# Scores and some values of a windowed attention on array tiles of 64 rows by 32 columns

## Chip, cores and metric

The kernel runs on one core of one Trainium2 chip. The metric is the device time of one execution in microseconds (us), the median of several runs. Beside them one execution was profiled; its times are those of the trace. The engines are named as in the profile: PE is the matrix engine (PEld its weight loads), DVE the vector engine, ACT the scalar engine, POOL the general one, SP the one that issues most transfers.

## The reference

Two layers follow each other, for 8 batches of 576 positions. The first is causal attention with 8 heads of 64, in which each position sees itself and the 127 before it, with a slope per head that falls with the distance. The second is a gated network that mixes positions.

```
scores = q @ k.T / sqrt(64) - slope[h] * |i - j|     # q, k, v: 8 batches, 8 heads, 576 x 64
scores = where(0 <= i - j < 128, scores, -1e9)
x = softmax(scores) @ v                              # heads side by side: 576 x 512
h = gelu(x @ w_in); u, g = h[:, :512], h[:, 512:]
g = w_sg @ layernorm(g) + b_sg                       # over positions
out = x + (u * g) @ w_out
```

## The kernel before

The work of the attention is cut into 32 pairs of heads (class `Pair`, number n, four to a batch). A pair's 576 queries are nine blocks of 64 (R = 64). The operands of the products of the attention are 32-bit floats, and the trace has two weight loads and two products for each call of `nc.tensor.matmul` on them.

**Scores.** `qk` holds q and k transposed: the 64 numbers of head 0 on partitions 0 to 63, those of head 1 on 64 to 127. One product of `score` has 64 queries of one head as weights and the keys that they can see as the moving operand: 192 columns, 128 for the second block of queries, 64 for the first. So it uses 64 rows and 64 columns of the array of 128 by 128, a quarter ("64*64" in the profile). `score_list(t2)` makes eight products (i, half, j) for two banks of PSUM, `banks[half]`; head j goes to the partitions `heads[half ^ j]`, so that four products in a row lie on four different quarters. For t2 = 0 it appends the two products of the first block ("last products" below), which go to bank 0 as well. From pair 5 on, one step `*` issues both t2 = 0 (banks from the pool `ps_a`) and t2 = 2 (banks from `ps_s`): 18 products, 36 in the trace. Before that the steps `a` and `c` issue them apart. `burst` keeps the order in which the list has them.

**Minima.** For each bank DVE runs `minima` (steps A, B, C, G): `copy_predicated` (L302) merges the two halves of a diagonal block, and `shift` (helper line L295) adds the slopes and takes the minimum of a row. Step A, of the bank with the last products, comes first. ACT takes exponentials (L311), DVE the inverse sums, POOL or ACT scales, PE transposes (L347, L360), and DVE multiplies with the mask into `px` (L356).

**Values.** `values` (step V, L384 and L388) multiplies by v: `part(k, c)` for the nine blocks k of keys, and `first(c)` for the first block of queries, each for the two halves of the columns of v. Odd k use rows 0 to 63 of the array and bank `x1[0]`, even k rows 64 to 127 and bank `x1[1]`; the half c picks the columns. These are quarters too, 20 products, 40 in the trace. A product has 192 columns for k = 1 to 6, 128 for k = 0 and 7, 64 for k = 8 and for `first`. For the pairs in `BEHIND` (13 and 15 to 29) the result of `first` goes into a bank of the scores of pair n + 2, and the two `first` lie on different rows; for the other pairs from 4 on both lie on rows 0 to 63, and before that on rows 64 to 127. In the order of steps, the values of pairs 15 to 29 come directly behind the scores of pair n + 2 on PE; those of pair 13 have other products between.

**Order.** Each step runs where the string `ORDER` puts it, and every engine takes its instructions in that order; a `Planner` checks the buffers. The rest of PE's work is the gated network, in products on the whole array (128*128), of which most go to `ps_m` (two buffers).

## Time and profile before

| | |
|---|---|
| median of 3 runs | 577.24 us (577.07 to 577.51) |
| the profiled execution, its own time | 576.7 us |
| its span from first to last instruction | 575.0 us |
| instructions | 14661, of them 5495 products and 5495 weight loads on PE |

A product's duration in the trace runs from its issue to its last result, so neighbours overlap; PE's share of busy time says only that it has something in flight. How long a stretch takes is read from the start of its first product to the start of the first product of the next work.

### The profile page before, as it was taken

To read this page: it belongs to the slowest core of one execution; us is meant where nothing else is said; L and a number is where in the kernel's file an instruction comes from. 1 tells how busy PE (TensorE), PEld (TensorE's weight loads), DVE (VectorE), ACT (ScalarE), POOL (GpSimd) and SP (SyncE) were. 2 spreads that over 40 slices of the span, in tenths; PEclk is the share of its full clock that TensorE was granted. 3 is DMA by queue.
4 is the path that set the end of the run, shared out by engine and by line. 5 is a ranking of instruction groups with operands and counts; after the bars stand their busy time and mean duration, and the time that the engine had idled before them with its cause. 6 is when DMAs were issued, how large, how long until landed. Compare 5 with 4: busy or idle time off the path is not lost.

```text
span 575.0 us, 14661 instructions
## 1 busy us (share of the span) xinstructions
PE 560.0 (97%) x5495; PEld 510.0 (89%) x5495; DVE 474.0 (82%) x1324; ACT 378.3 (66%) x1063; POOL 307.2 (53%) x365
## 2 busy tenths in 40 slices
PE   5899999999999999999999999999999999999997
PEld 4677899998899789998999998998999999998997
DVE  8989998799989778999787987878897988575646
ACT  7998997466844867567777576646695666733422
POOL 3676646520436544575338753496348653576325
PEclk9899999999999999999999999999999999999999
DMA  8675213216404413554260554136431606012502
GB/s 301 194 231 200 79 57 104 68 68 224 166 38 149 133 38 99 163 186 120 65 218 1 166 180 175 42 103 183 124 112 65 216 1 198 2 39 93 172 1 82
DMA packets 43561, 69.78 MB, mean 121 GB/s; under 512 B 3554, under 2 KB 31202, under 8 KB 43492
## 3 DMA queue, kind: packets, MB, share of 16 engines
q1 hardware_dynamic: 43492, 68.86, 36.7%
q8 instruction: 43, 0.70, 0.5%
q14 instruction: 26, 0.21, 0.1%
HBM read 56.27 MB, written 12.58 MB: 120 GB/s over the span
## 4 chain that ended last, share of the span: by engine, by line
PE 89%; DVE 4%; ACT 4%; DMA 2%; issue 1%; POOL 0%; SPq 0%; DVEq 0%; ACTq 0%
PE ps_m L609 13%; PE ps_m L1061 13%; PE ps_m L611 12%; PE ps_m L610 12%; PE ps_m L907 12%; PE ps_a L347 5%; PE ps_a L278 4%; PE ps_s L278 4%; PE ps_m L384 3%; PE ps_s L384 3%; PE ps_m L942 2%; PE ps_m L943 2%; ACT e L311 1%; PE ps_m L798 1%; PE ps_m L800 1%; DMA wst<-w_in 1%
## 5 line engine op out<-in xcount | busy, mean ns | idle before, releaser
L334 POOL TENSOR_TENSOR e<-e,rr 128x256 f32<-128x256 f32 (+2 forms) x116 | 80.6, 717 | 96.4 <-DVE rr L323 84.0
L311 ACT ACTIVATE e<-e,stats 128x128 f32<-128x128 f32 (+1 forms) x288 | 110.7, 387 | 17.2 <-DVE stats L295 16.6
L224 POOL TENSOR_TENSOR region<-u,region 128x288 fp32r<-128x288 f32 (+1 forms) x78 | 77.7, 1016 | 44.5 <-ACT region L1008 16.2
L356 DVE TENSOR_TENSOR px<-ps_a,m_both 128x1024 f32<-128x1024 f32 x64 | 77.4, 1216 | 5.4 <-PE ps_a L347 4.7
L609 PE MATMUL ps_m<-ws,region 128*128 128x288 f32 x256 | 78.3, 306 | 0.0
L611 PE MATMUL ps_m<-ws,region 128*128 128x288 f32 x256 | 75.9, 296 | 0.0
L610 PE MATMUL ps_m<-ws,region 128*128 128x288 f32 x256 | 75.6, 295 | 0.0
L732 POOL TENSOR_TENSOR rs<-rs,mhalf 128x1 f32<-128x1 f32 (+1 forms) x40 | 30.2, 756 | 57.5 <-DVE rs L729 57.3
L218 POOL TENSOR_TENSOR xs<-xf,xs 128x288 fp32r<-128x288 f32 (+1 forms) x48 | 49.9, 1060 | 13.8 <-ACT xs L403 13.8
L311 ACT ACTIVATION_READ_ACCUMULATOR e<-e,stats 128x1 f32 x288 | 54.5, 189 | 0.0
L1008 ACT ACTIVATE region<-u 128x576 fp32r<-128x576 f32 x35 | 23.7, 684 | 43.1 <-PE ps_m L610 17.5
L609 PEld LDWEIGHTS ps_m<-ws,region 128*128 128x128 f32 x256 | 48.3, 189 | 1.6 <-issue 0.8
L610 PEld LDWEIGHTS ps_m<-ws,region 128*128 128x128 f32 x256 | 48.3, 189 | 0.1
L611 PEld LDWEIGHTS ps_m<-ws,region 128*128 128x128 f32 x256 | 48.1, 188 | 0.2 <-DVE region L744 0.2
L609 PE MATMUL ps_m<-wi,xs 128*128 128x512 f32 x112 | 46.7, 417 | 0.1
L1068 DVE TENSOR_TENSOR xf<-ps_m,xf 128x576 f32<-128x576 f32 x48 | 35.8, 750 | 10.4 <-PE ps_m L1061 9.7
L611 PE MATMUL ps_m<-wi,xs 128*128 128x512 f32 x112 | 44.3, 396 | 0.0
L610 PE MATMUL ps_m<-wi,xs 128*128 128x512 f32 x112 | 44.2, 395 | 0.0
L347 PE MATMUL ps_a<-ident,e 128*128 128x128 f32 x256 | 38.6, 277 | 1.0 <-DVE px L356 1.0
L948 DVE TENSOR_TENSOR u<-ps_m,u 128x576 f32<-128x576 f32 x32 | 24.0, 753 | 18.2 <-PE ps_m L943 11.6
L278 PE MATMUL ps_s<-qk 64*64 64x192 f32 (+2 forms) x576 | 32.2, 338 | 5.5 <-DMA qk<-qkT 4.6
L295 DVE CUSTOM_DVE_ANT_0 e<-ps_s,bias 128x128 f32<-128x128 f32 (+1 forms) x140 | 34.9, 287 | 2.5
(217 smaller groups left out, 1591.8 us busy)
## 6 DMA issues: line engine op xcount, KB each, us to landing
qk<-qkT SPq DMA_DIRECT2D x32, 576.0 KB, 4.9
sum<-store SPq DMA_DIRECT2D x36, 512.0 KB, 4.7
outT<-xf SPq DMA_DIRECT2D x31, 288.0 KB, 3.0
vt<-v_in SPq DMA_DIRECT2D x32, 256.0 KB, 4.2
wst<-w_in SPq DMA_DIRECT2D x8, 512.0 KB, 5.2
store<-sum SPq DMA_DIRECT2D x6, 512.0 KB, 2.8
vt<-v_in SPq DMA_DIRECT2D x64, 32.0 KB, 3.8
wst<-w_out SPq DMA_DIRECT2D x4, 512.0 KB, 3.6
```

What stands on the lines that cost most here:

```text
L218: (engine or nc.gpsimd).tensor_tensor(out[:, cs], a[:, cs], b[:, cs], op)
L224: nc.gpsimd.tensor_tensor(out[:, fs], a[:, fs], b[:, fs], ALU.subtract)
L278: return lambda: nc.tensor.matmul(banks[half][to, c:c + k1 - k0], qk[js, 0, q0:q0 + R], qk[js, 1, k0:k1], start=True, stop=True)
L311: nc.scalar.activation(x, x, AF.Exp, bias=self.nm[0:n, i:i + 1], scale=-1.0, accum_out=self.sm[0:n, i:i + 1])
L334: nc.gpsimd.tensor_tensor(x[:, z:z + step, :], y[:, z:z + step, :], self.rr[0:n, i + z:i + z + min(k, step)].rearrange("p (m o) -> p m o", ...
L347: burst([lambda t=t: nc.tensor.transpose(cv[:, t // 2, t % 2], self.pr[j][:, t, :].rearrange("p (h c) -> p h c", h=2), ident[:, j * R:j * ...
L356: nc.vector.tensor_tensor(xv, cv, mv, ALU.mult)
L609: nc.tensor.matmul(dst, ah, bh, start=(first and i == 0), stop=False)
L610: nc.tensor.matmul(dst, ah, bl, start=False, stop=False)
L611: nc.tensor.matmul(dst, al, bh, start=False, stop=(last and i == n - 1))
L907: nc.tensor.matmul(dst, left(n, g, c)[:, ms], right(n, h, c), start=first and c == 0 and k == 0, stop=c == 1 and k == 2, skip_group_check= ...
L1061: nc.tensor.matmul(dst, p, q, start=first and f == 0 and k == 0, stop=f == 1 and k == 2, skip_group_check=True)
```

## The change

`score` makes two products of each: 32 queries as weights, so 64 rows by 32 columns of the array, an eighth. The half z of a block sees the keys from `q0 + z - 128` (or 0) to `q0 + z + 32`, so the moving operand has 160 columns and not 192; the second block of queries has 96 and 128, and not 128. The 32 queries of z = 32 are put 32 columns further, so a band of scores is now 160 columns behind the one before it, and `minima` reads it through `window`, a pattern of two pieces, of the same sizes as before. For t2 = 0 the order is i = 1, then i = 0, and the last products are taken out of the list and issued at the end of the step's burst (in `*`, behind those of t2 = 2).

In `values` the pairs of `BEHIND` cut c in four, so each product has 32 columns of v as weights and the same moving columns as before; the other pairs keep quarters. The order of k is 1 to 7, then 0, and k = 8 is issued between the `first` products. Nothing else changes; the order of steps is the same.

```diff
     XW = 2 * S + R
+    BAND = 5 * R // 2
+    LEAD = 2 * BAND + R // 2
+
+    def window(bank, c0, c1):
+        x = bank[:, c0:c0 + R].rearrange("p (t c) -> p t c", t=1)
+        return bass.AP(tensor=x.tensor, offset=x.offset, ap=[x.ap[0], [c1 - c0, 2], x.ap[2]])
...
         def scores(self, *t2s):
-            burst([x for t2 in t2s for x in self.score_list(t2, ps_a if len(t2s) > 1 and t2 == 0 else ps_s)])
+            insts = [x for t2 in t2s for x in self.score_list(t2, ps_a if len(t2s) > 1 and t2 == 0 else ps_s)]
+            burst(insts + (self.last_scores if 0 in t2s else []))
...
-            def score(half, j, c, q0, k0, k1):
-                js, to = heads[j], heads[half ^ j]
-                return lambda: nc.tensor.matmul(banks[half][to, c:c + k1 - k0], qk[js, 0, q0:q0 + R], qk[js, 1, k0:k1], start=True, stop=True)
+            half_block = R // 2
+
+            def score(half, j, c, q, k0, k1):
+                js, to = heads[j], heads[half ^ j].start + q % R
+                return lambda: nc.tensor.matmul(banks[half][to:to + half_block, c:c + k1 - k0], qk[js, 0, q:q + half_block], qk[js, 1, k0:k1], start=True, stop=True)
 
             insts = []
-            for i in range(2):
+            for i in (1, 0) if t2 == 0 else (0, 1):
                 for half in range(2):
                     for j in range(2):
-                        q0 = (2 * t2 + 1 + i + 2 * half) * R
-                        if q0 < P:
-                            insts.append(score(half, j, i * W + R, q0, 0, P))
-                        else:
-                            insts.append(score(half, j, i * W, q0, q0 - P, q0 + R))
+                        for z in (0, half_block):
+                            q0 = (2 * t2 + 1 + i + 2 * half) * R
+                            lo = max(q0 + z - P, 0)
+                            insts.append(score(half, j, i * BAND + lo - q0 + P, q0 + z, lo, q0 + z + half_block))
             if t2 == 0:
-                insts += [score(0, j, 2 * W, 0, 0, R) for j in range(2)]
+                self.last_scores = [score(0, j, LEAD, z, 0, R) for j in range(2) for z in (0, half_block)]
             return insts
...
-            nc.vector.copy_predicated(sv[:, 0:6:5, :], sel_first if alone else sel, sv[:, 2:4, :])
+            nc.vector.copy_predicated(window(bank, 0, BAND + P), sel_first if alone else sel, window(bank, P, BAND))
...
-            WIDE = D
-            cols = [c for j in (1, 0) for c in range(j * D, (j + 1) * D, WIDE)]
-            burst([part(k, c) for k in (0, 1, 2 * T, *range(2, 2 * T)) for c in cols] + [first(c) for c in cols])
+            wide = D // 2 if behind else D
+            order = [*range(1, 2 * T), 0, 2 * T]
+            cols = [c for j in (1, 0) for c in range(j * D, (j + 1) * D, wide)]
+            burst([part(k, c) for k in order[:-1] for c in cols] + [x for c in cols for x in (first(c), part(2 * T, c))])
```

## Rows read from the trace of the kernel before

**Rows 1.** The page: busy time, share of the span and instructions of each engine.
```profile
PE 560.0 (97%) x5495; PEld 510.0 (89%) x5495; DVE 474.0 (82%) x1324; ACT 378.3 (66%) x1063; POOL 307.2 (53%) x365
```

**Rows 2.** The page: the chain that ended last, share of the span by engine.
```profile
PE 89%; DVE 4%; ACT 4%; DMA 2%; issue 1%; POOL 0%; SPq 0%; DVEq 0%; ACTq 0%
```

**Rows 3.** Waits of PE: us in total, times, longest; longest first.
```profile
PE ps_s L278 <- DMA qk<-qkT: 4.6, 1, 4.6
...
PE ps_a L347 <- DVE px L356: 1.0, 1, 1.0
```

**Rows 4.** Windows: length, then busy us (and instructions) of PE, PEld, DVE, ACT, POOL.
```profile
0.00:30.00 30.00, 21.29 (x220) 16.78 (x220) 25.93 (x112) 26.39 (x91) 15.69 (x27) 0.94 0.75 248
...
400.00:500.00 100.00, 100.00 (x992) 93.41 (x991) 82.05 (x238) 70.72 (x192) 51.52 (x77) 1.00 0.35 112
```

**Rows 5.** Timeline of PE, one step of scores: start, us, what, count.
```profile
229.14 0.29 PE L943 MATMUL ps_m<-wsB,vB 66*128 66x288 f32 x1
229.37 0.88 PE L278 MATMUL ps_a<-qk 64*64 64x128 f32 x20
230.08 0.82 PE L278 MATMUL ps_s<-qk 64*64 64x192 f32 x16
230.83 0.40 PE L609 MATMUL ps_m<-ws,region 128*128 128x288 f32 x1
```

**Rows 6.** Timeline of PE, scores with values directly behind.
```profile
253.02 0.88 PE L278 MATMUL ps_a<-qk 64*64 64x128 f32 x20
...
254.38 1.48 PE L384 MATMUL ps_m<-px,vt 64*64 64x192 f32 x36
...
255.90 0.55 PE L347 MATMUL ps_a<-ident,e 128*128 128x128 f32 x3
```

**Rows 7.** Timeline of PE, values alone: two steps.
```profile
97.80 1.53 PE L384 MATMUL ps_s<-px,vt 64*64 64x128 f32 x36
...
99.27 0.44 PE L347 MATMUL ps_a<-ident,e 128*128 128x128 f32 x2
...
235.30 1.53 PE L384 MATMUL ps_m<-px,vt 64*64 64x128 f32 x36
...
236.87 0.40 PE L1061 MATMUL ps_m<-fifth,wo 128*128 128x288 f32 x1
```

**Rows 8.** Groups of PE by line and form: busy us, mean ns of one.
```profile
L384 PE MATMUL ps_m<-px,vt 64*64 64x192 f32 x408 | 25.3, 323 | 0.0
...
L384 PE MATMUL ps_m<-px,vt 64*64 64x64 f32 x68 | 4.8, 217 | 0.0
...
L278 PE MATMUL ps_m<-qk 64*64 64x192 f32 x28 | 3.0, 527 | 0.0
```

**Rows 9.** Timeline of PE, the first part of scores that are issued apart.
```profile
61.00 0.88 PE L278 MATMUL ps_s<-qk 64*64 64x128 f32 x20
61.81 0.40 PE L609 MATMUL ps_m<-xs,wi 128*128 128x288 f32 x1
```

**Rows 10.** Groups of PE by line and form, from 230.07 to 230.10 alone.
```profile
L278 PE MATMUL ps_s<-qk 64*64 64x192 f32 x4 | 0.3, 324 | 0.0
```

**Rows 11.** Timeline of PE from 230.07 to 230.10.
```profile
230.08 0.34 PE L278 MATMUL ps_s<-qk 64*64 64x192 f32 x4
```

**Rows 12.** Lines L278 and L384 from 262 to 263.5: ns, first and last start.
```profile
L278 PEld LDWEIGHTS ps_a<-qk x20: 129/133/133, 262.2 to 262.9; 64*64 64x64 f32 x20
...
L384 PEldq EVENT_SEMAPHORE  x1: 706/706/706, 262.8 to 262.8; - x1
```

**Rows 13.** Timeline of DVE behind the same scores.
```profile
230.33 0.30 DVE L302 COPY_PREDICATED ps_a<-sel,ps_a 128x128 f32<-128x128 uint8 x1 [1.16 <-PE ps_a L278]
...
233.01 0.75 DVE L948 TENSOR_TENSOR u<-ps_m,u 128x576 f32<-128x576 f32 x1
...
234.86 0.76 DVE L948 TENSOR_TENSOR u<-ps_m,u 128x576 f32<-128x576 f32 x1 [0.35 <-PE ps_m L943]
```

## The prediction

> **What bounds the kernel now.** I read the page's busy shares and its chain first, then the waits, then stretches, and last single bursts. The reader is to see in the first two that PE is both the busiest engine and the one on which 89% of the chain lies [rows 1, 2]. A busy PE proves little by itself, so the waits come next: what other engines made PE wait for is a few us, the most of it the first transfer [rows 3]. The windows say when: in the first 30 us PE is busy for 21, later for all of the time, while DVE has about 18 us of 100 idle and ACT and POOL more [rows 4]. So from about 30 us on, time taken off PE comes off the span, as long as the others keep up; in the first 30 us it mostly doesn't.

> The change touches only the bursts of lines L278, L384 and L388. A duration there is no cost, because products on different quarters run side by side. The cost of a burst is from its first start to the first start of what follows. I call it its slot:

> - scores of one step (`*`), 36 instructions: 230.83 - 229.37 = 1.46 us [rows 5]. There are 12 such bursts, all within 0.01 us of this.
> - scores with values behind, 76 instructions: 255.90 - 253.02 = 2.88 us [rows 6]. There are 15, of which 14 have this slot and one 2.95.
> - values alone: 99.27 - 97.80 = 1.47 us in 11 bursts of the 16 on quarters, and 236.87 - 235.30 = 1.57 us for pair 13 [rows 7].
> - five pairs issue their scores in two parts; one of them runs after 30 us, its first part in 0.81 us [rows 9].

> **What a slot is made of.** A product of 192 columns lasts 323 ns and one of 64 columns 217 ns, so a column costs 106 / 128 = 0.83 ns [rows 8], and, with two instructions to a product, 1.66 ns per column of a product. Now take the columns that fall on the busiest quarter. Scores: bank 0 has 128 + 192 + 64 on a quarter for t2 = 0 and twice 192 for t2 = 2, which is 768; bank 1 has four times 192, also 768. 768 x 1.66 = 1.27 us, so 0.19 us of the slot is the first weight load, steps between products and the way to the next work. Values on quarters: 3 x 192 + 128 + 64 + 64 = 768 on all rows, 1.27 + 0.19 = 1.46 against 1.47 measured. Pair 13: rows 64 to 127 with the first half of v have 832, 1.38 + 0.19 = 1.57, as measured. Scores and values together: at most 768 + 832 = 1600, 2.65 + 0.19 = 2.84 against 2.88. The model holds within 0.04 us in all four, so I use it for the change.

> **Scores on eighths.** Each product splits in two on different columns of the array, and each half has 160 columns. The busiest eighth now has, for t2 = 0, 160 + 128 + 64 and for t2 = 2 twice 160, 672 in all; those of bank 1 have 640. If eight run side by side, a slot falls by (768 - 672) x 1.66 = 0.16 us. For the five pairs in two parts it is the same sum; the four in the first 36 us lie where PE waits for others, or where products still take 527 ns for 192 columns [rows 4, 8]. I take nothing for them, and up to 1.3 us (4 x 0.32 at half speed) as the bound.

> **Values.** Cutting c in four doubles the instructions and leaves the columns on each eighth as they were on the quarter, so values alone gain nothing: 832 for pair 13, 768 for those on quarters from pair 4 on. The order of k, long ones first, pairs 192 with 192, 128 with 128 and 64 with 64 on the two sets of rows; the slot without any loss between is already within 0.01 us of the model, so this is 0, at most 16 x 0.02 = 0.3 us. Directly behind scores it counts together: the busiest eighth has 640 + 832 = 1472 (the next 672 + 768 = 1440), against 1600. That is 128 x 1.66 = 0.21 us less.

> **Sum on PE.** 13 x 0.16 + 15 x 0.21 = 2.1 + 3.2 = 5.3 us.

> Weight loads: one of 32 columns should take less than one of 64, but eight have to be started before all eighths run, not four; I take zero for the two together, and 0.03 us per burst either way as the bound (four starts within 0.02 us, below), which is 30 x 0.03 = 0.9 us.

> **What the doubled instructions need.** A burst of scores now has 72 products and 72 loads for 1.30 us, and 152 and 152 with values for 2.67 us, one instruction in about 9 ns. Does PE get and start them so fast? Starts: four products of 324 ns lie within 0.34 us, so four started in 0.02 us, about 5 ns apart [rows 10, 11]. That shows that a start is cheap, not that it stays so for 152. Supply: near 262 us PE stood still, and its sequencer passed the wait that stands behind all 36 products and 36 loads of the scores at 262.8 us, 0.6 us after the first of them began at 262.2 [rows 12]. So 72 instructions took at most 0.6 to 0.7 us, 8 to 10 ns each with the waits among them. 304 x 10 = 3.0 us is the worst that this row allows, where 2.67 is wanted and 2.88 is the slot now. I take it as hidden, because the row is only an upper bound and part of a burst is queued before it begins; the bound costs the 15 joint bursts 0.37 us each, 5.5 us.

> **DVE.** The copies and shifts keep their sizes. But step A waits for the last products, and they now end the burst. Before, they ended with the group of 20 at 229.37 + 0.88 = 230.25 [rows 5], and A began at 230.33, after DVE had stood idle for 1.16 us [rows 13]. Now the columns of the busiest eighth take 1.12 us; the last instruction starts 0.05 before their end, with some 0.08 of the 0.19 us of loads and steps ahead of it, and lasts 0.22 us [rows 8]: 229.37 + 1.12 - 0.05 + 0.08 + 0.22 = 230.74. So A is 0.49 us late. In 13 of the pairs from 4 on A begins within 0.16 us of these products; six more lose 0.1 to 0.3 us; in the others DVE comes later anyway. That is 7.3 us of lateness on DVE in all. Behind A on DVE stand, in this example, the release of a `ps_m` buffer at 233.01 (L948), for which PE's next block of products waits, and 0.35 us of idle time at 234.86 which takes most of the delay up again [rows 13]. The bound is 0 to 7.3 us. As DVE made PE wait only singly before, 1.0 us at the most [rows 3], its results mostly come early, and I take 0.8 us back.

> **The number.** The profiled execution took 576.7 us, its span 575.0, with 1.7 outside it, which stays. 576.7 - 5.3 + 0.8 = 572.2. The median of the runs is 0.5 above the profiled execution, so 572.7 us.

> [...]

> **Rivals.**
> 1. *Eighths don't run denser than quarters do.* Today the highest lasting density is 76 products in 2.88 - 0.23 us, 35 ns each. If something (issue, the reading of four moving operands over the same rows, the loads) holds it there, the doubled number takes 152 x 35 = 5.3 us instead of 2.65 in the joint bursts and 72 x 35 = 2.5 instead of 1.27 in scores alone: 15 x 2.7 + 13 x 1.2 = 56 us more, 633 us. For it: no row has more than four side by side. Against it: starts 5 ns apart, and four that don't slow each other. It decides from 18 ns for each start on: (2.88 - 0.23) / 152. At 20 ns the kernel is already slower, 15 x 0.39 = 6 us and scores alone 13 x 0.17 = 2, about 585 us.
> 2. *The late step A comes back on PE.* If half of its 7.3 us or more ends as waits of PE, 3.7 to 7.3 of the 5.3 us are lost: 575.6 to 579.2 us. For it: 13 places where DVE stands ready. Against it: DVE is idle for 101 us of 575 [rows 1], and PE's results for the others come no later than before.
> 3. *More is gained.* The early pairs (1.3 us), the order of the values (0.3), shorter loads (0.9) and no loss to DVE: 576.7 - 5.3 - 2.5 = 568.9, 569.4 as a median.
> 4. *The supply of instructions eats it.* At the bound of 10 ns the joint bursts don't shrink but grow by 0.12 us (1.8 in all), and only the 2.1 us of scores alone stay: 576.7 - 2.1 + 1.8 + 0.8 = 577.2, 577.7 as a median, no change.

> **How the numbers follow.** The sum as worked out 0.66 (570.3 to 574.7: the unknown small terms on one side, up to 2.5 more to DVE on the other), rival 1 0.11, rival 2 0.13, rival 3 0.05, rival 4 0.05. The range that holds 8 in 10 leaves out rival 1 and the outer ends of rivals 2 and 3, 0.16 in all: 569.5 to 577.8 us. Changes under 0.2% (1.15 us, about what a measurement of this kernel can tell from none) are same: half of rival 4 and a third of rival 2, 0.08 with a little of the others. Slower: rival 1 and a bit of rival 2, 0.12. Faster 0.80.

> **What will show it.** Right: 64*32 products at 192 or fewer columns with eight in flight, slots of 1.30 us for scores, 2.67 for scores with values, 1.47 for values alone; the first L302 about 0.5 us later after the start of the scores, and PE's waits on DVE hardly longer. Wrong by rival 1: slots of 2 us and more, with starts evenly spaced by 18 ns or more. By rival 2: slots as forecast, but new waits of PE for L948, L302 or L1068. By rival 4: gaps in the later part of a joint burst only. The forecast also falls if a product of 160 columns on an eighth lasts longer than 217 + 96 x 0.83 = 297 ns.

## The result

The change made the kernel slower: 580.75 us median of 4 runs (580.54 to 581.35) against 577.36 before, a ratio of 1.0061 [1.0045, 1.0077]. 572.7 was forecast, with a range to 577.8. The profiled execution took 580.61 us, its span 578.9, where before it was 575.0.

The page of the changed kernel: busy times, the chain, and the queue that brings instructions (packets, MB, share). The last row read "43, 0.70, 0.5%" before.
```profile
PE 557.2 (96%) x7287; PEld 509.1 (88%) x7287; DVE 473.2 (82%) x1324; ACT 378.5 (65%) x1063; POOL 308.4 (53%) x365
...
q8 instruction: 57, 0.93, 0.6%
...
PE 83%; DVE 9%; ACT 3%; DMA 2%; issue 2%; POOL 1%; SPq 0%; DVEq 0%; POOLq 0%
```
Against [rows 1, 2] PE is busy for 2.8 us less, and yet the span is 3.9 us longer. The chain says where to look: PE's share fell from 89% to 83%, DVE's rose from 4% to 9%, and "issue" (time in which an engine waits for nothing that the view can name) from 1% to 2%. In both kernels this queue has a packet of 16 KB for each 256 loads and products of PE (0.93 MB / 57 = 16 KB; 2 x 7287 / 57 = 256, 2 x 5495 / 43 = 256).

The timeline of PE, the same scores alone as in [rows 5], and of DVE behind them, as in [rows 13]:
```profile
230.58 0.46 PE L286 MATMUL ps_a<-qk 64*32 64x160 f32 x10
...
231.64 0.30 PE L286 MATMUL ps_a<-qk 64*32 64x64 f32 x7
231.87 0.40 PE L617 MATMUL ps_m<-ws,region 128*128 128x288 f32 x1
```
```profile
232.03 0.29 DVE L308 COPY_PREDICATED ps_a<-sel,ps_a 128x128 f32<-128x128 uint8 x1 [1.65 <-PE ps_a L286]
```
The slot is 1.29 us instead of 1.46. Step A begins 232.03 - 230.58 = 1.45 us after the scores began, before 0.96. PE is 0.17 us ahead, DVE 0.49 us behind.

Scores with values behind, an ordinary burst of the changed kernel (compare [rows 6]):
```profile
432.98 0.75 PE L286 MATMUL ps_a<-qk 64*32 64x160 f32 x29
...
434.04 0.24 PE L286 MATMUL ps_a<-qk 64*32 64x64 f32 x4
434.09 0.34 PE L391 MATMUL ps_m<-px,vt 64*32 64x192 f32 x1
434.10 0.23 PE L286 MATMUL ps_a<-qk 64*32 64x64 f32 x2
...
434.15 1.40 PE L391 MATMUL ps_m<-px,vt 64*32 64x192 f32 x59
...
435.79 0.40 PE L617 MATMUL ps_m<-ws,region 128*128 128x288 f32 x1
```
435.79 - 432.98 = 2.81 us (2.82 in 12 of 15, and one of 2.90) instead of 2.88. Two are much longer, 3.98 and 3.32 us. The longer of them, near its end:
```profile
256.80 0.22 PE L395 MATMUL ps_s<-p,vt 64*32 64x64 f32 x1
257.85 0.21 PE L391 MATMUL ps_m<-px,vt 64*32 64x64 f32 x1 [0.84 <-issue]
...
258.20 0.33 PE L354 MATMUL ps_a<-ident,e 128*128 128x128 f32 x1
```
PE starts nothing for 1.05 us in the middle of a row of products that wait for no one: no semaphore ends the gap, so the view calls it "issue".

Waits of PE from 250 us to 560 us and from 36 us to 250 us, us in total, times, longest. Before, these stretches held one transfer of 0.2 us, and three waits of 0.4 to 0.9 us of which none was for POOL, `u`, `px` or `stats`. Left out below is one of 1.1 us at 198.8 us, which the view calls "issue" (L915); before, the same place (L907) had 0.9 us.
```profile
PE ps_m L391 <- issue: 0.8, 1, 0.8
...
PE ps_a L354 <- DVE stats L302: 0.4, 1, 0.4
```
```profile
PE ps_m L617 <- DVE u L956: 0.7, 1, 0.7
...
PE ps_a L354 <- POOL e L341: 0.5, 1, 0.5
PE ps_a L367 <- DVE px L363: 0.5, 1, 0.5
```

**The account.** From the timelines of both kernels I took the first start of each burst and of what follows it, from the first burst behind 48 us to the last product, and summed the slots by kind and what lies between them. The columns are differences from before in us, for the changed kernel and for the runs told of below; the 13 bursts of values alone stay within 0.07 us everywhere and are left out. "Start" is how much later than before the first of these bursts began; "to the end" is the sum from there on. These columns come from the one profiled execution of each kernel, which lies up to 1.2 us from the median of its runs, in e8 4.0; the last column is the ratio of medians, each against runs of the kernel before made beside it.

| kernel | start | scores alone (14) | with values (15) | between | to the end | time / before |
|---|---|---|---|---|---|---|
| changed | +0.11 | -1.31 | +0.70 | +4.57 | +3.93 | 1.0061 |
| e1 last products behind t2 = 0 | +0.21 | -0.91 | +2.52 | +2.48 | +4.06 | 1.0055 |
| e2 before, last products moved | +0.84 | +0.66 | +0.12 | +4.71 | +5.52 | 1.0103 |
| e3 changed, values on quarters | -0.01 | -1.44 | -0.09 | +4.01 | +2.43 | 1.0041 |
| e4 both of e1 and e3 | +0.06 | -0.90 | +1.28 | +0.64 | +0.97 | 1.0018 |
| e5 last products first, values on quarters | +1.06 | -2.20 | -0.18 | +1.39 | -1.04 | 0.9991 |
| e6 last products first, values on eighths | +0.95 | -2.23 | +1.55 | +2.79 | +2.09 | 1.0023 |
| e7 eighths only where no values follow | +0.44 | -2.06 | -0.03 | +3.02 | +0.92 | 1.0039 |
| e8 = e1, code shifted | +8.46 | -0.82 | +3.24 | +1.65 | +4.04 | 1.027 |
| e9 = e6 with small transfers | +0.87 | -2.23 | -0.78 | +1.54 | -1.50 | 0.9966 |
| e10 = e5 with small transfers | +0.60 | -2.12 | +0.17 | +0.96 | -1.05 | 0.9976 |
| e11 = e6, four pairs on quarters | +0.33 | -2.15 | +2.20 | +1.07 | +1.10 | 1.0016 |

In the changed kernel the loss is between the bursts (4.57 us), and in the joint bursts a gain that doesn't come. Of the 12 bursts of scores alone 10 are 0.17 us shorter; that the sum is 1.31 and not 2.2 is one of 2.01 us, at whose end PE waited for `u` of L956, and one of 1.48.

### The profile page after: what moved, and what is told of

The parts are those of the page before. It is cut to its first block, busy times and chain, and to the rows that moved or that the text cites. A ratio compares the mean times of both kernels' runs of the same rounds, so it can differ in the third digit from the quotient of the medians.

```text
span 578.9 us, 18232 instructions
## 1 busy us (share of the span) xinstructions
PE 557.2 (96%) x7287; PEld 509.1 (88%) x7287; DVE 473.2 (82%) x1324; ACT 378.5 (65%) x1063; POOL 308.4 (53%) x365
## 4 chain that ended last, share of the span: by engine, by line
PE 83%; DVE 9%; ACT 3%; DMA 2%; issue 2%; POOL 1%; SPq 0%; DVEq 0%; POOLq 0%
PE ps_m L1069 12%; PE ps_m L915 12%; PE ps_m L617 12%; PE ps_m L619 11%; PE ps_m L618 11%; PE ps_a L354 5%; PE ps_m L391 4%; PE ps_s L391 3%; PE ps_a L286 3%; PE ps_s L286 2%; DVE e L302 2%; PE ps_m L950 1%; PE ps_m L951 1%; ACT e L318 1%; PE ps_m L806 1%
## 5 line engine op out<-in xcount | busy, mean ns | idle before, releaser
L956 DVE TENSOR_TENSOR u<-ps_m,u 128x576 f32<-128x576 f32 x32 | 24.0, 752 | 17.1 <-PE ps_m L951 10.5
L286 PE MATMUL ps_s<-qk 64*32 64x160 f32 (+3 forms) x1152 | 32.4, 305 | 5.5 <-DMA qk<-qkT 4.5
L302 DVE CUSTOM_DVE_ANT_0 e<-ps_s,bias 128x128 f32<-128x128 f32 (+1 forms) x140 | 34.9, 287 | 2.5
```

What stands on the lines that cost most here:

```text
L286: return lambda: nc.tensor.matmul(banks[half][to:to + half_block, c:c + k1 - k0], qk[js, 0, q:q + half_block], qk[js, 1, k0:k1], start=Tru ...
```

## The experiments

Two theories stood at first. A: the last products at the end of the burst make step A late, DVE passes this on, and PE waits. B: with eighths PE runs out of instructions in the joint bursts.

**e1, last products back behind t2 = 0**, all on eighths.
```diff
-            insts = [x for t2 in t2s for x in self.score_list(...)]
-            burst(insts + (self.last_scores if 0 in t2s else []))
+            insts = []
+            for t2 in t2s:
+                insts += self.score_list(...)
+                insts += self.last_scores if t2 == 0 else []
+            burst(insts)
```

> The changed kernel, with the products of the first block of queries issued directly behind those of t2 = 0 again, not at the end of the burst. Theory A (the late first copy L302 makes DVE late, and DVE then makes PE wait): most of the 4.8 us that PE loses in the stretches between the bursts comes back, so about 576 us (575 to 577). Theory B (the loss lies in the joint bursts, where PE runs out of instructions): nothing comes back, 580 to 581 us. In both the slots of scores alone stay at 1.29 us.

580.05 us, 1.0055 [1.0041, 1.0069]. The stretches between bursts lose 2.1 us of their 4.57, as A wants, and the chain's DVE share is back at 5%. But scores alone take 1.39 us instead of 1.29, because four short products now stand in the middle, and four joint bursts are 0.4 to 2.0 us longer than the others, with gaps called "issue" that add up to 2.9 us with one behind a burst. (One of the four, of 3.22 us at 265, is another case: its gap of 0.16 us stands before the first product of the values, behind a semaphore wait of 0.68 us.) One loss went and another came; neither theory alone holds.

**e2, the kernel before with only the last products moved to the end.**
```diff
-            burst([x for t2 in t2s for x in self.score_list(...)])
+            insts = [x for t2 in t2s for x in self.score_list(...)]
+            burst(insts + (self.last_scores if 0 in t2s else []))
...
-                insts += [score(0, j, 2 * W, 0, 0, R) for j in range(2)]
+                self.last_scores = [score(0, j, 2 * W, 0, 0, R) for j in range(2)]
```

> The kernel before, with one thing of the change alone: the products of the first block of queries are issued at the end of the burst of scores; all on quarters, the values as before. Theory A: slower by 3 to 6 us, 580 to 583 us, since the copy comes 0.6 us later and no PE time is saved. Theory B: no change, 577 us.

582.71 us, 1.0103 [1.0089, 1.0117]: 5.8 us from the place of two products alone. Nearly all slots stay (1.46, 2.88, 1.47; one of scores alone takes 2.00 us, one 1.58, and one joint burst 3.04); 4.71 us lie between. Its waits of PE from 36 to 250 us, and its chain:
```profile
PE ps_a L348 <- POOL e L335: 1.6, 1, 1.6
...
PE ps_m L610 <- DVE u L949: 0.5, 1, 0.5
PE ps_a L361 <- DVE px L357: 0.4, 1, 0.4
```
```profile
PE 82%; DVE 10%; ACT 2%; issue 2%; DMA 1%; POOL 1%; SPq 0%; DVEq 0%; POOLq 0%
```
They are the waits of the changed kernel, for the same buffers. With one of 0.3 us for `stats` behind 250 us, those for POOL and DVE come to 2.8 us; the rest of the loss lies in stretches where the view names no gap of PE, and which wait it is there is not shown. That the place of the two products is the cause is shown by the edit: nothing else was changed. Theory A holds, for its part.

**e3, the changed kernel with `wide = D` for all values.**
```diff
-            wide = D // 2 if behind else D
+            wide = D
```

> The changed kernel with the values of all pairs on quarters, scores on eighths as they are. A joint burst has 36 instructions fewer on either side, and a change of tile shape between scores and values. Theory A: the joint slot is 1.29 + 1.47 = 2.76 us against 2.82, 15 x 0.06 = 0.9 us, so about 580 us. Theory B: the two long stalls in joint bursts (1.1 and 0.4 us) go as well, and the time is 578 us or less.

579.10 us, 1.0041 [1.0028, 1.0054]. No joint burst stands still and their sum is level with before; the slot is 2.88 us, not the 2.76 expected. So eighths for the values cost the changed kernel 580.75 - 579.10 = 1.65 us (1.2 by the two ratios to before) where they should have given 3. The late step A is still there (4.01 between).

**e4, both of these edits.**

> Both edits: the products of the first block in place again, and all values on quarters; scores stay on eighths, the order of the values stays the new one. Theory A: 575 to 576 us, below the kernel before; theory B: 578 us. If both hold and add up: 573.5 us.

578.21 us, 1.0018 [1.0008, 1.0027]. The stretches are almost those of before (+0.64), so the late A is gone, but the short products in mid-burst cost 0.10 us or a little more in each of 27 bursts: 1.39 and 2.97 us. That is 2.7 us, about what is missing from the 575 to 576 expected.

**e5, last products first**, the other half of the rows ahead in each step, values on quarters. Bank 0 is then complete as early as before, and the short products open the burst.
```diff
...
-            insts = []
-            for i in (1, 0) if t2 == 0 else (0, 1):
-                for half in range(2):
+            insts = [score(0, j, LEAD, z, 0, R) for j in range(2) for z in (0, half_block)] if t2 == 0 else []
+            for i in (1, 0) if t2 == 0 else (0, 1):
+                for half in (1, 0):
...
-            wide = D // 2 if behind else D
+            wide = D
```

> Scores of all pairs on eighths, values on quarters as before; the four last products (64 columns) open the burst and the other half of the rows goes ahead in each step, so that bank 0 is complete after t2 = 0 and step A is as early as before. Theory A (the late step A is the loss, and the last products in mid-burst cost the 0.10 us that the run with them after t2 = 0 showed because TensorE is short of instructions there): ahead, the queue is full, the scores alone take 1.29 to 1.31 us, the joint slot 2.87 to 2.90, the stretches between bursts are those of before, and the time is 2 us under before, 574.5 to 576. Rival (short products cost their 0.1 us wherever they stand): scores alone 1.39, joint 2.97, 577 to 578.5, as in the run with both.

576.50 us against 576.99, 0.9991 [0.9982, 1.0000]. Scores alone take 1.29 us and step A comes 0.91 us after their start. From e3 to e5 only the place of the last products and the order of the halves differ, and 2.6 us of time and 2.6 us between the bursts are gone. But of the 2.20 us that the scores gain, 1.39 come back between the bursts, 0.85 of it in five stretches that begin right behind such a burst: the one behind 115.17 us (114.79 before), for instance, is 0.29 us longer, 0.14 of it a new wait for DVE's `px`. The joint burst gains nothing:
```profile
429.16 0.81 PE L285 MATMUL ps_a<-qk 64*32 64x64 f32 x40
429.73 0.79 PE L285 MATMUL ps_s<-qk 64*32 64x160 f32 x32
430.45 1.42 PE L388 MATMUL ps_m<-px,vt 64*64 64x192 f32 x32
...
432.03 0.40 PE L614 MATMUL ps_m<-ws,region 128*128 128x288 f32 x1
```
The last scores end at 429.73 + 0.79 = 430.52, and the values begin only 0.07 us before that.

**e6, the same with values behind scores on eighths.** The edit is that of e5 without the change of `wide`. From the changed kernel it differs in the place of the last products and in the order of the halves.

> The same as the last-products-first kernel, but the values that follow scores are on eighths again, as in the changed kernel: only the place of the last products differs from it. Theory A with the supply of instructions: the late step A's 5 us come back, joint slot 2.82, so 575 to 576 by the slots alone, or 0.9 us under its sister with values on quarters. Theory B (bursts on eighths run dry when the next block of instructions is being fetched): one to five joint bursts stand still by 0.4 to 2 us, other ones than in the changed kernel, and the time is 1 to 4 us above its sister, 576 to 580.

578.73 us, 1.0023 [1.0013, 1.0034]. An ordinary joint burst:
```profile
433.26 0.79 PE L285 MATMUL ps_s<-qk 64*32 64x160 f32 x32
433.82 1.42 PE L388 MATMUL ps_m<-px,vt 64*32 64x192 f32 x64
...
435.41 0.40 PE L614 MATMUL ps_m<-ws,region 128*128 128x288 f32 x1
```
Here the values begin 0.23 us before the scores end, and the slot is 2.73 us in 12 of 15 bursts (2.82 in the changed kernel, 2.88 in e5). So the forecast of 2.67 is nearly reached where tiles of one size follow each other and no short products stand at the seam. Three bursts take 4.80, 3.36 and 3.99 us. The first of them:
```profile
255.45 0.23 PE L388 MATMUL ps_m<-px,vt 64*32 64x64 f32 x2
257.47 0.31 PE L392 MATMUL ps_s<-p,vt 64*32 64x64 f32 x4 [1.78 <-issue]
...
257.82 0.44 PE L351 MATMUL ps_a<-ident,e 128*128 128x128 f32 x2
```
The DMA view of 253 to 258 us: the busy share of the DMA engines in 40 slices, and the packets of the two queues.
```profile
DMA  7999999999998786820000000000000000000000
...
q1 hardware_dynamic: 414, 0.74, 39.1%
q8 instruction: 1, 0.02, 1.2%
```
One block of instructions comes in this window. The trace has its packet at 255.04, for 0.99 us: it starts as the data runs out that had kept the DMA engines at shares of 0.6 and more. In the changed kernel the packet is at 255.56, for 0.89 us, again at the end of such data, and PE goes on at 257.85. This made a third theory, C: the stalls are blocks of instructions that wait behind data.

**e7, eighths only in pairs whose scores stand alone**, in joint pairs all as before.
```diff
+            if self.n in BEFORE:
+                return self.score_quarters(t2, banks, qk, heads)
```
(with the copies, shifts and values of the kernel before for these pairs)

> Scores on eighths, last products first, only in the pairs whose scores stand alone (pairs 0 to 14 and 16); the pairs whose scores are followed by values have scores and values as the kernel before, order of values included. Theory A: scores alone 1.29 to 1.31 in place of 1.461 twelve times, joint slot 2.885 as before, no late step A: 2 us under before, 574.5 to 575.5. Rival (an earlier end of the scores is given back at the next wait for VectorE or the POOL engine, so that nothing of it reaches the end): stretches longer by as much as the bursts are shorter, 576.5 to 577.5.

579.18 us, 1.0039 [1.0021, 1.0057], but ten runs spread from 576.97 to 582.0. The slots are as expected (1.29 and 2.88); between the bursts the profiled one, of 577.94, lost 3.0 us, 1.4 of it where PE waited 1.5 us at 263.7. The view puts this wait down to ACT, which had long been done; the load of the scores' input, issued at 257.69, landed at 263.54 us, after 5.9 us, where 4.5 was the longest of the three from 225 to 275 us before. That explains one run, not the spread; this run decides nothing.

**e8, e1 with 64 small products more at the start**, to shift all later instructions against the bounds of the blocks.
```diff
+            if n == 12:
+                for i in range(64):
+                    nc.tensor.matmul(banks[0][:, 0:16], spare[:, 0:P], spare[:, 0:16], start=True, stop=True)
```

> The kernel with the last products after t2 = 0 and all eighths, with 64 more products of 16 columns on zeros among the idle ones at the start, while TensorE waits for its data: 128 instructions more ahead of everything else, half of a 16 KB block. Theory B (the long stalls in joint bursts, 4.85 us in place of 2.82 at 252.9 us of its sister, are waits for the next block of instructions): the stalls move to other bursts or change size by more than 0.5 us, those bursts that stood still at 252.9 and 417.5 are near 2.82, and the time changes by 1 to 4 us to either side of 580. Rival (the stalls belong to what these bursts do or to transfers under way at that time): the same bursts stand still by the same amounts, 580 within 0.6.

593.13 us, 1.027 [1.0236, 1.0304]. As a time it is spoiled: with the products, thought to be cheap, the bursts begin 8.46 us later than before (0.21 in e1), and the granted clock was 0.66 from 20 to 30 us (0.83 before). The stalls answer the question all the same. PE's waits behind 36 us:
```profile
PE ps_m L394 <- issue: 3.7, 2, 2.3
```
The bursts that take 4.85, 3.24 and 3.47 us in e1 are at 2.82 here; the one of 3.22 takes 5.32, and one at 489 us, which was at 2.82, takes 4.60. The stalls belong to the place of the code, not to the work.

**e9 and e10, e6 and e5 with small transfers.** The stores of the output write 32 columns of 288 or 576, the loads of the sums bring 32 of 1024.
```diff
-nc.sync.dma_start(sums[i].bitcast(F32), store[number][:, i])
+nc.sync.dma_start(sums[i].bitcast(F32)[:, 1, 1, 0:32], store[number][:, i, 1, 1, 0:32])
...
-nc.sync.dma_start(out[b, cs, :], x[c // 2][:, c % 2, :])
+nc.sync.dma_start(out[b, cs, 0:32], x[c // 2][:, c % 2, 0:32])
...
```

> The last-products-first kernel with values behind scores on eighths, and with the bulk transfers cut: the stores of the output write 32 of their 288 or 576 columns and the loads of the sums bring 32 of 1024 columns, so most of the output is left unwritten and its last batches are computed from other sums; every transfer still stands in its queue with its waits, and all work of the engines is done. Theory C (the long stalls in joint bursts are instruction blocks that wait behind data: each one's fetch started just as a stretch with all DMA engines full ended): no joint burst longer than 3.1 us, median slot 2.73, and the time is 1.5 to 2.3 us under its sister with values on quarters and the same cut, 573 to 575. Rival (a block that ends inside a joint burst is late whatever the traffic, because 304 instructions go by in 2.7 us): three to five joint bursts of 3.3 to 4.9 us remain, and it is level with its sister or up to 2 us above it.

> The last-products-first kernel with all values on quarters, and the same cut of the transfers (most of the output unwritten, sums not loaded in full): the control for the run above. It had no long stall in a joint burst before the cut, so both theories expect slots of 1.291, 2.876 and 1.468, and what the cut gives is only shorter waits for the loads of queries and keys: 0 to 1 us under 576.5, 575.5 to 576.5.

575.48 us, 0.9966 [0.9954, 0.9977], and 575.68, 0.9976 [0.9966, 0.9986]. PE executes the same loads and products in e6 and e9, but PE has 24 semaphore waits less (176 against 200), so the ends of the blocks fall 4 to 21 instructions later in the joint bursts. Of the three stalled bursts of e6 one is at 2.73 now and one at 2.96 instead of 3.36; the 0.5 us of "issue" behind another is gone. What was 2.2 us between e6 and e5 is -0.2. The traffic need not have done all of that: in the burst that is at 2.73 and in the one with the gap behind it the end of the block has moved 16 and 13 instructions on. In the other two it moved 6 and 4, and the gaps shrank, the longest from 2.0 to 1.3 us between starts. But this first stall stays, and theory C in its full form (none over 3.1 us) falls; of the three to five long bursts of its rival one is left, of 4.07 us:
```profile
255.40 0.22 PE L388 MATMUL ps_m<-px,vt 64*32 64x64 f32 x1
256.68 0.21 PE L388 MATMUL ps_m<-px,vt 64*32 64x64 f32 x1 [1.06 <-issue]
...
257.02 0.44 PE L351 MATMUL ps_a<-ident,e 128*128 128x128 f32 x2
```
The DMA view of 253 to 255 us of e9:
```profile
DMA  0000000000000000000000090000000000000000
...
q8 instruction: 1, 0.02, 3.4%
```
Nothing but the block moves here. Its packet starts at 254.18 and takes 1.08 us, and still PE stands still until 256.68. So this block was late in a joint burst on eighths even alone, and with data ahead of it, in e6, it was later (packet at 255.04, PE at 257.47). In e10 one joint burst takes 3.20 us where 2.88 was expected: its first product of the values stands behind a semaphore wait of 0.68 us, as in the burst of e1 at 265 us.

**e11, e6 with quarters for the values of four pairs** whose bursts, or the work right behind them, had stood still.
```diff
-            wide = D // 2 if behind else D
+            wide = D // 2 if behind and self.n not in (15, 19, 24, 25) else D
```

> A try at a version that beats both kernels: last products first, all scores on eighths, values behind scores on eighths except in pairs 15, 19, 24 and 25, whose joint bursts (or the work right behind) stood still in the run with all of them on eighths; all transfers in full. Eleven joint bursts of 2.73 and four of 2.88 in place of fifteen of 2.88 are 1.6 us less than the kernel with all values on quarters. If the stalls belong to the pairs that I changed, 574.5 to 575.5, under both kernels; if the blocks of instructions, whose bounds shift by 80 instructions with each changed pair, now end in other bursts while the DMA engines are full, new stalls of 0.5 to 2 us appear and it is 576 to 578.

578.50 us, 1.0016 [1.0005, 1.0028]. The four pairs are at 2.88 us; now others stand still, 5.64 us at 261 and 3.83 at 298.
```profile
PE ps_m L388 <- issue: 2.3, 2, 2.0
...
PE ps_s L392 <- issue: 0.8, 1, 0.8
```
This choice of pairs didn't help, and each choice moves the bounds of the blocks. e5 is the best found: better than the changed kernel, and not told apart from the kernel before.

## Why the prediction was wrong

**Scores alone: right.** 1.30 forecast, 1.29 measured, and e5 shows what they are worth at the end: of 2.2 us about 1.0 from there on, 0.5 in the medians, with an interval that reaches none. The reading that "time taken off PE comes off the span" held for half.

**Eight side by side: right.** In e5 32 products of 160 columns begin and end within 0.79 us, the last of them lasting 0.30 us, so starts are (0.79 - 0.30) / 31 = 16 ns apart, and a product lasts 296 ns in the narrow stretches, where 297 was the limit set (the changed kernel, at 231.04 us). Rival 1 is out. That eight would run so was an assumption of the forecast: the rows of before show four. A weight load of 32 columns, which the prediction took to be shorter, lasts 105 ns for the values (L391), where one of 64 lasts 133 (L384 before).

**The late step A: the step that failed.** Its lateness was worked out right, 0.49 us; its price was taken as 0.8 us out of 0 to 7.3. The runs say 5.8 us on quarters (e2) and, on eighths, where the scores themselves end 0.17 us earlier, 2.6 us (e3 to e5, which differ in the order of the halves as well) or 3.4 us between the bursts (e3 to e4, the place alone). The argument for 0.8 was that DVE idles 101 us in all and that PE had hardly waited for it. Windows of the kernel before, chosen around the later losses, show the fault (the columns are those of [rows 4]):
```profile
49.00:67.00 18.00, 17.50 (x156) 14.55 (x156) 16.70 (x65) 17.42 (x51) 11.45 (x12) 1.00 0.30 97
80.00:92.00 12.00, 12.00 (x138) 10.98 (x138) 11.51 (x48) 10.58 (x28) 4.81 (x4) 1.00 0.37 117
108.00:120.00 12.00, 12.00 (x138) 10.74 (x137) 10.15 (x51) 9.05 (x42) 4.72 (x5) 1.00 0.12 47
250.00:262.00 12.00, 11.96 (x129) 9.83 (x128) 11.03 (x33) 8.04 (x37) 6.98 (x7) 1.00 0.75 235
375.00:390.00 15.00, 15.00 (x169) 14.60 (x168) 13.13 (x35) 7.26 (x22) 14.65 (x19) 1.00 0.33 99
```
DVE is busy 16.70 of 18, 11.51 of 12 and 11.03 of 12 us in three of them, 92 to 96% where the mean of the span is 82%. There its idle time lies elsewhere, half a microsecond late isn't made up, and `u`, `px` and the scale on POOL behind it reach PE late (waits of 0.7, 0.5 and 0.5 us in the changed kernel). In the other two it is busy for 85 and 88%, and in the last POOL for 14.65 of 15 us, so DVE's own share doesn't explain every loss. That PE had not waited for DVE before was no sign of a reserve. Rival 2 named this mechanism, with a chance of 0.13; it was right in kind and nearly in size (3.7 to 7.3 us back; 4.57 measured, of which e5 has 1.39 without a late A).

**The joint bursts: a term mis-sized.** 15 x 0.21 = 3.2 us were forecast, and the sum came out at +0.70. Three parts: 0.06 us of each slot was never there (e6: 2.73, not 2.67); 0.09 us more (2.82) is put down to the four short products at the seam, where, unlike in e6, the values start among them, though the order of the halves differs from e6 too; and two bursts stood still for 1.1 and 0.5 us. (The slot that the prediction gives as 2.95 us is 265.18 - 262.26 = 2.92.)

**The supply of instructions: taken as hidden, and it wasn't.** Rival 4 priced a rate of 8 to 10 ns per instruction, the same in all bursts. Its sign, gaps in the later part of a joint burst only, came true, but what costs is the block behind the rate, and it costs single bursts. From the packets and the gaps: PE goes on 257.47 - 256.03 = 1.44 us after the packet's end in e6, 257.85 - 256.45 = 1.40 in the changed kernel, 256.68 - 255.26 = 1.42 in e9. With 0.99, 0.89 and 1.08 us for the packet itself that is 2.43, 2.29 and 2.50 us from the packet's start. A joint burst on eighths uses 304 instructions in 2.73 us, 9 ns each, 256 in 2.3 us. On quarters it is 152 in 2.88 us, and 256 last 4.9 us; in e5 it is 224, and 256 last 3.3. So, as an estimate from these rows, eighths in a joint burst use instructions about as fast as blocks can come.

A count over PE's records in the traces (loads, products and semaphore waits, in order of start) bears this out. In six kernels 15 gaps of 0.1 to 2.3 us, in a joint burst on eighths or right behind it, end at a record whose number is 193 or 194 modulo 256, in e8 too, where 128 more stand ahead. The record 256 before it lies 3 to 55 records behind the start of the burst, and the packet starts after the burst has begun. So PE stopped only where a burst, with the work right behind it, passes two ends of blocks; 144, 152 or 224 instructions are too few for that, and no such burst stopped so. Not every burst that passes two stops: in e6 those at 328.35 and 366.17 us don't, and their packets had started before them. PE goes on 2.3 to 2.8 us after the packet's start in all 15.

The queue of instructions has a row on the page of before (43 packets, 0.70 MB), which the prediction doesn't use.

In sum, from 49 us on: forecast -2.1 (scores), -3.2 (joint), +0.8 (DVE) = -4.5 us; measured -1.31, +0.70, +4.57 = +3.93 with the rest.

What stays open: what lies in the 1.4 us between the end of a packet and PE's next start, which no row shows; how many blocks PE holds at a time; when a block is asked for, and so how long a stall gets (in e9 the packet started only 125 records before the place where PE stopped, with no data ahead of it); how much of the loss between bursts is which wait; and the spread of e7.

## What to carry to other kernels

## What the hardware showed that was not expected

- A joint burst was 0.15 us longer with a change of the tile size inside it: values on quarters behind scores on eighths begin 0.07 us before the last scores end, on eighths 0.23 us (e5, e6), and the slots are 2.88 and 2.73 us. Values alone are no shorter on eighths (pair 13: 1.61 us in e6, 1.58 in e5).
- PE stood still for 0.1 to 2.3 us with no semaphore and no engine to blame (the 15 gaps in six kernels); the sign was "issue" within a row of equal products or right behind it, with one packet on the instruction queue that started 2.3 to 2.8 us before PE went on. "Issue" at the first product of another kind was a semaphore wait in e1 and e10 (0.68 us in both).
- Four products of 64 columns cost 0.10 us in the middle of a burst of scores (1.39 against 1.29), and nothing at its start or end. Before values on quarters they cost nothing either (2.88 in e3 and e5); before values on eighths the slot is 0.09 us longer with them (2.82 against 2.73), with the order of the halves changed as well.
